# Identity first, two-transfer B loads, last values in three pieces, unequal output halves: four small changes to a decode-attention kernel that is bound by its DMA stream

## The chip, the cores and the metric

The kernel runs on one core of one Trainium2 chip. The metric is the device time of one execution in microseconds (us); the profile's span, from the first instruction to the last, is about 1.8 us shorter. The time before was 440.04 us, median of 3 runs (439.99 to 440.07).

## The reference, cut to what matters

Two attention layers decode one token each for a batch of 4, with 32 query heads, 8 key/value heads and head size 128. Layer A attends to all 8192 cached positions, layer B to the last 2048. The results stand side by side in the output.

```python
# A: whole cache; B: the same with k_cache[:, :, Sk-W:], v_cache[:, :, Sk-W:], W = 2048
q = (x @ wq).reshape(B, Sq, Hq, Dh)...           # B=4, Sq=1, D=512, Hq=32, Dh=128
scores = einsum("bhqd,bhkd->bhqk", q, k) * Dh**-0.5
o = einsum("bhqk,bhkd->bhqd", softmax(scores), v)
return o.reshape(B, Sq, Hq*Dh) @ wo
```

Nearly all bytes are the two caches, read once: 184.6 MB from HBM in all.

## The kernel before

The work is cut into 20 units, each with 4 MiB of keys and 4 MiB of values: first 4 of layer B (one per batch entry, all 8 heads), then 16 of layer A (one batch entry and two heads). K and V have two slots each. All large loads are issued by SyncE (SP) in one order: query weights of B and A, K(0), then K(u), V(u-1) in turn, at the end the last values and the last output weights (Wl). The cuts are marked by "...".

```python
# GpSimd's fills, in program order
op("pool", pool_mask0, inc=("mk0",)); op("pool", pool_mask1, inc=("mka",))
def pool_setup0(pool):
    ...memset onesf, onesb, RQ, OT_sb, oacc, PT, Wo_sb...
op("pool", pool_setup0, waits=[("mk0",), ("mka",)], inc=("pset",))
def pool_setup1(pool): ...affine_select ident, identf...
op("pool", pool_setup1, waits=[("pset",)], inc=("setup",))
...
# loads of a B unit: four transfers of 1 MiB, 128 partitions each
for q in range(NSEG):
    src = bass.AP(..., ap=[[TS * DH, 64], [SK * DH, 2], [1, TS * DH]])
    w = [("T", tjob_idx[(u - 2, 4 * q + 3)])] if u >= 2 else []      # keys
    op("sp", dma(buf[:, slot, q * TS:(q + 1) * TS, :], src), waits=w, ...)
...
# the tail: last unit's weighted values (PV) in 8 groups, each waits for its piece of V
VCH = [2, 2, 2, 1, 1]             # pieces of 1, 1, 1, 0.5, 0.5 MiB
for c in range(NC):
    if c == 4: pe_SM(L); ...seed the two output halves with oacc...
    pe_PV(L, c, bank=KTB[0], waits=[("VL", vch_of[c])])
...
H2 = D // 2                       # final projection: 8 heads x 2 halves
for hq in range(8):
    for hf in (1, 0): matmul(out=halves[hf], ..., rhs=Wl_sb[:, hq, hf*H2:(hf+1)*H2])
vector copies half 0 -> SyncE sends it; scalar copies half 1 -> ScalarE sends it
for i in range(3): sp.wait_ge(out i landed)
```

## Time and profile before

| | before |
|---|---|
| device time, median | 440.04 us |
| profile span | 438.2 us |
| read from HBM | 184.56 MB, 421 GB/s over the span |
| the big DMA queue's packets, share of 16 engines' span | 99.2% |
| TensorE busy | 83% |

From the profile page: the row of DMA busy tenths and of GB/s in 40 equal slices of the span, the packet line, and the line of the big queue.

```profile
DMA  8999999999999999999999999999999999999996
GB/s 336 432 413 422 419 419 420 421 446 406 447 431 431 416 445 431 431 431 431 431 431 431 431 431 431 431 431 431 405 456 431 431 428 431 434 431 407 449 404 256
DMA packets 13396, 184.75 MB, mean 422 GB/s; under 512 B 1428, under 2 KB 2504, under 8 KB 4552
...
q1 hardware_dynamic: 13296, 184.56, 99.2%
```

The DMA engines are full (9 tenths) in every slice but the first and last (8 and 6 tenths). From these rows I estimate that nothing that the compute engines do in between moves the end, as long as they ask for the next load in time.

Busy times by stretch (start and end in us, length, then busy us and instruction counts of PE, PEld, DVE, ACT and POOL, then granted clock, DMA share, GB/s). The first stretch holds the loads of B units, the second those of A units:

```profile
34.00:92.00 58.00, 54.97 (x1044) 51.72 (x1047) 30.59 (x56) 29.91 (x32) 2.24 (x7) 1.00 1.02 422
110.00:390.00 280.00, 241.19 (x4630) 223.97 (x4636) 143.35 (x298) 129.15 (x137) 12.83 (x47) 0.95 1.01 431
```

B's packets are 8 KB, A's are 32 KB. The start, from the timeline (start us, length us, engine, line, operation, output and inputs, count, and in brackets the idle time before and what ended it):

```profile
5.43 3.51 POOL L538 MEMSET Wo_sb<- 128x4096 bf16 x1
19.43 0.28 POOL L542 TENSOR_SCALAR_AFFINE_SELECT ident<-onesb 128x128 bf16<-128x128 bf16 x1 [10.49 <-issue]
...
20.74 3.56 PE L221 MATMUL KT<-xT,V_sb 128*128 128x4 bf16 x128 [0.37 <-ACT xT L204]
...
24.33 4.90 SPq L567 DMA_DIRECT2D V_sb<-in_B_v_cache_dram  x4
```

GpSimd fills until about 9 us, shows no instruction for 10.5 us, and then makes the identity matrix (`ident`, with which TensorE transposes). The first projections on TensorE wait for it. The first values load of B goes out at 24.33 us, behind them.

The tail, from the timeline. L324 is PV, L700 the final projection, L705 and L704 the copies of the two output halves:

```profile
422.99 3.91 PE L324 MATMUL OT<-PT,V_sb 128*128 128x64 bf16 x128 [0.64 <-DMA V_sb<-in_A_v_cache_dram]
...
428.23 1.98 PE L324 MATMUL KT<-PT,V_sb 128*128 128x64 bf16 x64 [1.33 <-issue]
...
431.55 2.10 PE L324 MATMUL KT<-PT,V_sb 128*128 128x64 bf16 x64
433.69 0.18 DVE L489 TENSOR_TENSOR OT_sb<-KT,RL 128x8 bf16<-128x8 f32 x1 [2.05 <-PE KT L324]
...
433.97 0.27 PE L700 MATMUL KT<-Wl_sb,OT_sb 128*4 128x256 bf16 x1 [0.31 <-issue]
...
435.75 0.27 PE L700 MATMUL KT<-Wl_sb,OT_sb 128*4 128x256 bf16 x1
...
436.05 0.37 ACT L705 ACTIVATE osb<-KT 4x256 bf16<-4x256 f32 x1 [9.71 <-PE KT L700]
436.16 0.41 DVE L704 CAST osb<-SA 4x256 bf16<-4x256 f32 x1 [2.30 <-PE SA L700]
436.46 0.27 ACTq L567 DMA_DIRECT2D out_dram<-osb  x1
436.60 0.28 SPq L567 DMA_DIRECT2D out_dram<-osb  x1
```

PV of the last unit but one starts when its values have landed (422.94 us in the trace's semaphore records). PV of the last unit runs in two stretches of four groups without a visible wait. Then come 16 projection matmuls, two copies, two output transfers. The projection waits a little for its weights, from the waits list (engine, line, releaser, total us, times, longest):

```profile
PEld KT L700 <- DMA Wl_sb<-in_A_wo_dram: 0.6, 3, 0.2
```

### The profile page before, as it was taken

What the parts mean: (1) busy time and instruction counts of PE and PEld (TensorE: products, weight loads), DVE (VectorE), ACT (ScalarE), POOL (GpSimd) and SP (SyncE); (2) the same over time, 40 slices, a digit from 0 to 9 for tenths busy, and PEclk for the clock granted to TensorE, in tenths of its full rate; (3) what the DMA queues carried; (4) which work ended last, traced back from release to release, by engine and by line L of the source; (5) the groups of instructions that cost most, each with busy time, mean ns of one, the idle gap of its engine ahead of it and who ended that gap; (6) DMA issues with size and microseconds to landing.
All of it is one profiled execution on the core that took longest, in us unless ns stands there. A gap on an engine that the chain in (4) does not pass through costs nothing.

```text
span 438.2 us, 15448 instructions
## 1 busy us (share of the span) xinstructions
PE 363.7 (83%) x7134; PEld 336.2 (77%) x7144; DVE 207.8 (47%) x423; ACT 193.3 (44%) x217; POOL 29.1 (7%) x96
## 2 busy tenths in 40 slices
PE   0168898998998959896989598969878895989996
PEld 0158897997997949795979588868868794979975
DVE  0003455664574634563456246625644563456651
ACT  1024473573653625371635254434635361536530
POOL 7200000000000000000000000000100000000000
PEclk9999999999999997999899699989998999799999
DMA  8999999999999999999999999999999999999996
GB/s 336 432 413 422 419 419 420 421 446 406 447 431 431 416 445 431 431 431 431 431 431 431 431 431 431 431 431 431 405 456 431 431 428 431 434 431 407 449 404 256
DMA packets 13396, 184.75 MB, mean 422 GB/s; under 512 B 1428, under 2 KB 2504, under 8 KB 4552
## 3 DMA queue, kind: packets, MB, share of 16 engines
q1 hardware_dynamic: 13296, 184.56, 99.2%
q8 instruction: 8, 0.13, 0.1%
q14 instruction: 4, 0.03, 0.0%
q0 software_dynamic: 64, 0.02, 0.0%
q10 hardware_dynamic: 24, 0.01, 0.0%
HBM read 184.56 MB, written 0.01 MB: 421 GB/s over the span
## 4 chain that ended last, share of the span: by engine, by line
PE 51%; DMA 43%; issue 2%; SPq 2%; DVE 1%; PEld 1%; PEldq 0%
DMA K_sb<-in_A_k_cache_dram 29%; PE KT L277 25%; PE OT L324 10%; DMA K_sb<-in_B_k_cache_dram 7%; DMA V_sb<-in_A_v_cache_dram 7%; PE SB L308 4%; PE SA L308 4%; PE KT L388 4%; SPq L567 1%; PE SA L336 1%; DVE oacc L396 1%; PE KT L324 1%; PEld OT L324 1%; PE KT L260 0%; DVE OS L493 0%
## 5 line engine op out<-in xcount | busy, mean ns | idle before, releaser
L277 PE MATMUL KT<-identf,K_sb 128*128 128x128 f32 x1280 | 207.2, 295 | 46.2 <-DMA K_sb<-in_A_k_cache_dram 34.2
L286 ACT ACTIVATE KT_sb<-KT 128x1024 bf16<-128x1024 bf16 x160 | 163.4, 1025 | 123.0 <-PE KT L277 123.0
L277 PEld LDWEIGHTS KT<-identf,K_sb 128*128 128x128 f32 x1280 | 146.9, 149 | 51.5 <-DMA K_sb<-in_A_k_cache_dram 35.2
L285 DVE COPY KT_sb<-KT 128x512 int32<-128x512 int32 x160 | 110.5, 691 | 154.6 <-PE KT L277 153.2
L324 PE MATMUL OT<-PT,V_sb 128*128 128x64 bf16 x2560 | 78.1, 193 | 1.9 <-issue 1.3
L324 PEld LDWEIGHTS OT<-PT,V_sb 128*128 128x128 bf16 x2560 | 75.9, 98 | 2.1 <-issue 1.4
L461 ACT ACTIVATE PT<-Dt 128x512 bf16<-128x512 f32 x40 | 24.6, 632 | 84.1 <-DVE Dt L450 84.1
L308 PEld LDWEIGHTS SA<-RQc,KT_sb 128*128 128x128 bf16 x1280 | 56.9, 98 | 2.3
L308 PEld LDWEIGHTS SB<-RQc,KT_sb 128*128 128x128 bf16 x1280 | 51.1, 97 | 7.9 <-issue 4.4
L308 PE MATMUL SA<-RQc,KT_sb 128*128 128x16 bf16 x1280 | 56.3, 170 | 0.0
L308 PE MATMUL SB<-RQc,KT_sb 128*128 128x16 bf16 x1280 | 52.8, 170 | 0.0
L412 DVE TENSOR_REDUCE M<-SB 128x8 f32<-128x512 f32 (+1 forms) x20 | 13.8, 692 | 49.9 <-PE SB L308 49.9
L433 POOL PARTITION_ALL_REDUCE MB<-M1m x20 | 7.7, 387 | 335.1 <-DVE M1m L426 335.1
L388 PE MATMUL KT<-Wo_sb,OL 128*4 128x512 bf16 x80 | 18.9, 379 | 0.0
L198 PE MATMUL KT<-ident,x_sb 4*128 4x4 bf16 x8 | 0.5, 169 | 20.1 <-POOL identf L544 20.1
L198 PEld LDWEIGHTS KT<-ident,x_sb 4*128 4x128 bf16 x8 | 0.4, 111 | 20.3 <-issue 20.3
L468 DVE TENSOR_REDUCE LB<-SA 128x8 f32<-128x512 f32 (+1 forms) x20 | 13.7, 684 | 2.8 <-PE SA L336 2.8
L450 DVE TENSOR_TENSOR Dt<-SA,MBm 128x512 f32<-128x512 f32 x20 | 13.8, 691 | 0.7
L412 DVE TENSOR_REDUCE M<-SA 128x8 f32<-128x512 f32 (+1 forms) x20 | 13.6, 681 | 0.0
L450 DVE TENSOR_TENSOR Dt<-SB,MBm 128x512 f32<-128x512 f32 x20 | 13.6, 681 | 0.0
L336 PE MATMUL SA<-PT,onesb 128*128 128x128 bf16 x168 | 12.7, 218 | 0.0
L388 PEld LDWEIGHTS KT<-Wo_sb,OL 128*4 128x4 bf16 x80 | 6.0, 84 | 8.1
(73 smaller groups left out, 122.2 us busy)
## 6 DMA issues: line engine op xcount, KB each, us to landing
K_sb<-in_A_k_cache_dram SPq DMA_DIRECT2D x15, 4096.0 KB, 22.7
V_sb<-in_A_v_cache_dram SPq DMA_DIRECT2D x15, 4096.0 KB, 30.6
K_sb<-in_B_k_cache_dram SPq DMA_DIRECT2D x16, 1024.0 KB, 22.0
V_sb<-in_B_v_cache_dram SPq DMA_DIRECT2D x16, 1024.0 KB, 18.4
V_sb<-in_B_wq_dram SPq DMA_DIRECT2D x1, 4096.0 KB, 12.4
V_sb<-in_A_wq_dram SPq DMA_DIRECT2D x1, 4096.0 KB, 21.8
Wo_sb<-in_B_wo_dram SPq DMA_DIRECT2D x4, 1024.0 KB, 12.0
K_sb<-in_A_k_cache_dram SPq DMA_DIRECT2D x2, 2048.0 KB, 17.6
```

Source lines behind the costliest of these rows:

```text
L277: ins = pe.transpose(out=bkf[:, pi * 128:(pi + 1) * 128], in_=K_sbf[:, slot, t0:t0 + 2, :].rearrange("p t d -> p (t d)"), identity=identf[ ...
L285: return e.tensor_copy(out=KT_sb.bitcast(I32)[:, tj % NKT, :], in_=bkf.bitcast(I32)[:, :])
L286: return e.activation(out=KT_sb[:, tj % NKT, :], in_=bk[:, :], func=ACTF.Copy)
L308: ins = pe.matmul(out=stb[:, t % NTH * C:(t % NTH + 2) * C], lhsT=ktv[:, pi, :, e], rhs=RQc[:, u % 2, t // TS, e, :], start=(e == 0), stop ...
L324: ins = pe.matmul(out=otb[:, s * NW:s * NW + w], lhsT=V_sb[:, slot, t, :], rhs=PT[:, slot, t * C:t * C + w], start=(j == 0), stop=(j == n ...
L336: ins = pe.matmul(out=SA[u % 2][:, s * NM:(s + 1) * NM], lhsT=onesb[:, :], rhs=PT[:, u % 2, c0:c0 + NM], start=(i == 0), stop=(i == n - 1))
L388: ins = pe.matmul(out=bk[0:Bn, 0:D], lhsT=OL[:, i // REP, i % REP, :], rhs=Wo_sb[:, i // REP, i % REP, :], start=(i == 0), stop=(i == C - 1))
L412: return dve.tensor_reduce(out=M1[:, h * n:(h + 1) * n].rearrange("p (s h) -> p s h", h=C), in_=bank[:, :].rearrange("p (s j h) -> p s h j ...
L433: return pool.partition_all_reduce(MB[:, 0:n], M1m[:, 0:n], channels=128, reduce_op=ReduceOp.max)
L450: return dve.tensor_tensor(out=Dt[:, h * NTH * C:(h + 1) * NTH * C].rearrange("p (s j h) -> p s j h", s=Sh, h=C), in0=bank[:, :].rearrange ...
L461: return act.activation(out=PT[:, u % 2, a:b], in_=Dt[:, a:b], func=ACTF.Exp, scale=scale)
L468: return dve.tensor_reduce(out=LB[:, 0:n].rearrange("p (s h) -> p s h", h=C), in_=SA[u % 2][:, 0:NSEG * NM].rearrange("p (s j h) -> p s h ...
```

## The change

The intent, as far as the diff shows it: start TensorE's first work earlier; issue fewer DMAs and so fewer semaphore writes (1,429 packets of 4 bytes in the trace before); end with fewer and larger packets; and balance the two output copies, as VectorE's took 0.41 us and started later than ScalarE's 0.37 us.

```diff
-        op("pool", pool_mask0, ...); op("pool", pool_mask1, ...)
         def pool_setup0(pool):
             pool.memset(dummy...); pool.memset(onesf...)
-            pool.memset(onesb...), RQ[0], RQ[1], OT_sb, oacc, PT, Wo_sb
-        op("pool", pool_setup0, waits=[("mk0",), ("mka",)], inc=("pset",))
+            return pool.memset(onesb[:, :], 1.0)
+        op("pool", pool_setup0, inc=("ones",))
-        op("pool", pool_setup1, waits=[("pset",)], inc=("setup",))
+        op("pool", pool_setup1, waits=[("ones",)], inc=("setup",))
         op("pool", pool_perm, ...)
+        pool_zero: RQ[0], RQ[1], OT_sb, oacc, PT, Wo_sb -> ("pset",); then pool_mask0, pool_mask1
+        (the two consumers of these fills wait for "pset")
...
-        VCH = [2, 2, 2, 1, 1]
+        VCH = [4, 2, 2]
-        H2 = D // 2
+        H2 = 3 * D // 8          # half 0: 192 columns, half 1: 320
...
-                for q in range(NSEG):
-                    src ... ap=[[TS * DH, 64], [SK * DH, 2], [1, TS * DH]]
-                    keys wait for T(u-2, 4q+3)
+                for hh in range(2):
+                    src ... ap=[[TS * DH, 64], [2 * SK * DH, NSEG], [1, TS * DH]]
+                    dst = partitions hh, hh+2, ..., all four segments
+                    keys wait for T(u-2, 15)
...
-            for i in range(3):
+            for i in (1, 2, 0):
                 sp.wait_ge(out i landed)
```

(cut to its core)

More of the change, by code (lines that the diff above doesn't have):

```diff
@@ L125, in bass_concat_heads__gqa_block_cached__sliding_block_cached__decode_kernel @@
                  "out0", "out1", "out2", "Tq", "Td", "Ta", "S", "PV", "Ed", "Ea", "Eq", "vs", "sub", "exp", "otr", "otp",
-                 "ocp", "Ef", "fin0", "fin1", "ar1", "SM", "pset", "setup", "pm0", "pm1", "oc", "ocB", "mk0", "mk", "mka", "perm", "rq"]
+                 "ocp", "Ef", "fin0", "fin1", "ar1", "SM", "ones", "pset", "setup", "pm0", "pm1", "oc", "ocB", "mk0", "mk", "mka", "perm", "rq"]
         sems = {n: sm("s_" + n) for n in names}
@@ L250, in efn @@
                 return ins
-            add(dict(eng="act", fn=efn, waits=[("T", idx)], inc=("E", idx)))
+            add(dict(eng="act", fn=efn, waits=[("T", idx), ("pset",)], inc=("E", idx)))
         def pe_filler(n):
@@ L512, in pool_otp @@
             return dict(eng="pool", fn=lambda pool: pool.tensor_copy(out=OTp[:, :, :], in_=OT_sb[:, P, q, :, :]), waits=w, inc=("otp", tn))
-        def pool_mask0(pool):
-            mkv = MK[:, :].rearrange("p (g s h) -> p g s h", g=NSEG, s=2)
-            pool.memset(mkv[0:64, :, 0, :], 0.0)
-            pool.memset(mkv[0:64, :, 1, :], -BIG)
-            pool.memset(mkv[64:128, :, 0, :], -BIG)
-            return pool.memset(mkv[64:128, :, 1, :], 0.0)
-        op("pool", pool_mask0, inc=("mk0",))
-        def pool_mask1(pool):
-            pool.memset(MASK[0][0:64, 0:REP], 0.0)
-            pool.memset(MASK[0][0:64, REP:C], -BIG)
-            pool.memset(MASK[0][64:128, 0:REP], -BIG)
-            return pool.memset(MASK[0][64:128, REP:C], 0.0)
-        op("pool", pool_mask1, inc=("mka",))
         def pool_setup0(pool):
@@ L531, in pool_setup0 @@
             pool.memset(onesf[:, :], 1.0)
-            pool.memset(onesb[:, :], 1.0)
-            pool.memset(RQ[0][:, :, :, :, :], 0.0)
-            pool.memset(RQ[1][:, :, :, :, :], 0.0)
-            pool.memset(OT_sb[:, :, :, :, :], 0.0)
-            pool.memset(oacc[:, :], 0.0)
-            pool.memset(PT[:, :, :], 0.0)
-            return pool.memset(Wo_sb[:, :, :, :], 0.0)
-        op("pool", pool_setup0, waits=[("mk0",), ("mka",)], inc=("pset",))
+            return pool.memset(onesb[:, :], 1.0)
+        op("pool", pool_setup0, inc=("ones",))
         def pool_setup1(pool):
@@ L555, in bass_concat_heads__gqa_block_cached__sliding_block_cached__decode_kernel, with pool_zero, pool_mask0, pool_mask1 @@
         op("pool", pool_perm, waits=[("setup",)], inc=("perm",))
+        def pool_zero(pool):
+            pool.memset(RQ[0][:, :, :, :, :], 0.0)
+            pool.memset(RQ[1][:, :, :, :, :], 0.0)
+            pool.memset(OT_sb[:, :, :, :, :], 0.0)
+            pool.memset(oacc[:, :], 0.0)
+            pool.memset(PT[:, :, :], 0.0)
+            return pool.memset(Wo_sb[:, :, :, :], 0.0)
+        op("pool", pool_zero, inc=("pset",))
+        def pool_mask0(pool):
+            mkv = MK[:, :].rearrange("p (g s h) -> p g s h", g=NSEG, s=2)
+            pool.memset(mkv[0:64, :, 0, :], 0.0)
+            pool.memset(mkv[0:64, :, 1, :], -BIG)
+            pool.memset(mkv[64:128, :, 0, :], -BIG)
+            return pool.memset(mkv[64:128, :, 1, :], 0.0)
+        op("pool", pool_mask0, waits=[("pset",), ("perm",)], inc=("mk0",))
+        def pool_mask1(pool):
+            pool.memset(MASK[0][0:64, 0:REP], 0.0)
+            pool.memset(MASK[0][0:64, REP:C], -BIG)
+            pool.memset(MASK[0][64:128, 0:REP], -BIG)
+            return pool.memset(MASK[0][64:128, REP:C], 0.0)
+        op("pool", pool_mask1, inc=("mka",))
         for sh in range(2):
@@ L580, in bass_concat_heads__gqa_block_cached__sliding_block_cached__decode_kernel @@
             pe_job_perm(P)
-        op("pe", None, waits=[("E", perm_idx[0]), ("setup",)])
+        op("pe", None, waits=[("E", perm_idx[0]), ("pset",)])
+        op("pool", None, waits=[("mka",)])
         add(pool_rq(0))
@@ L672, in bass_concat_heads__gqa_block_cached__sliding_block_cached__decode_kernel @@
         turn[0] = None
-        H2 = D // 2
-        halves = [SA[(L + 1) % 2][0:Bn, 0:H2], KTB[2][0:Bn, 0:H2]]
+        H2 = 3 * D // 8
+        HS = [(0, H2), (H2, D)]
+        halves = [SA[(L + 1) % 2][0:Bn, 0:H2], KTB[2][0:Bn, 0:D - H2]]
         def pe_seed(pe):
@@ L678, in pe_seed @@
             for hf in range(2):
-                ins = pe.matmul(out=halves[hf], lhsT=identf[0:Bn, 0:Bn], rhs=oacc[:, hf * H2:(hf + 1) * H2], start=True, stop=False)
+                ins = pe.matmul(out=halves[hf], lhsT=identf[0:Bn, 0:Bn], rhs=oacc[:, HS[hf][0]:HS[hf][1]], start=True, stop=False)
             return ins
@@ L699, in lfn @@
                     def lfn(pe, hq=hq, hf=hf):
-                        return pe.matmul(out=halves[hf], lhsT=OT_sb[:, 0, NSEG - 1, hq, :], rhs=Wl_sb[:, hq, hf * H2:(hf + 1) * H2],
+                        return pe.matmul(out=halves[hf], lhsT=OT_sb[:, 0, NSEG - 1, hq, :], rhs=Wl_sb[:, hq, HS[hf][0]:HS[hf][1]],
                                          start=False, stop=(hq == C - 1))
@@ L715, in kv_load @@
             if un["P"] == 1:
-                for q in range(NSEG):
-                    base = cache[un["b"], 2 * q, SK - W:SK, :]
-                    src = bass.AP(tensor=base.tensor, offset=base.offset, ap=[[TS * DH, 64], [SK * DH, 2], [1, TS * DH]])
-                    if kind == "K":
-                        w = [("T", tjob_idx[(u - 2, 4 * q + 3)])] if u >= 2 else []
-                    else:
-                        w = [("otr", u - 2)] if u >= 2 else [("T", tjob_idx[(1, 1)])] if u else [("T", qp_idx[(1, NQP - 1)])]
-                    op("sp", dma(buf[:, slot, q * TS:(q + 1) * TS, :], src), waits=w, inc=(kind if q == NSEG - 1 else kind + "h", u, q))
+                if kind == "K":
+                    w = [("T", tjob_idx[(u - 2, NJ - 1)])] if u >= 2 else []
+                else:
+                    w = [("otr", u - 2)] if u >= 2 else [("T", tjob_idx[(1, 1)])] if u else [("T", qp_idx[(1, NQP - 1)])]
+                for hh in range(2):
+                    base = cache[un["b"], hh, SK - W:SK, :]
+                    src = bass.AP(tensor=base.tensor, offset=base.offset, ap=[[TS * DH, 64], [2 * SK * DH, NSEG], [1, TS * DH]])
+                    dst0 = buf[:, slot, :, :]
+                    pstr = dst0.ap[0][0]
+                    dst = bass.AP(tensor=dst0.tensor, offset=dst0.offset + hh * pstr, ap=[[2 * pstr, 64], [TS * DH, NSEG], [1, TS * DH]])
+                    op("sp", dma(dst, src), waits=w, inc=(kind, u, hh))
                 return
@@ L736, in kv_load @@
             sem = sem_of((kind, u))
-            op("sp", lambda sp: sp.sem_inc(sem, 48), waits=w, bump=(sem, 48, None))
+            op("sp", lambda sp: sp.sem_inc(sem, 16), waits=w, bump=(sem, 16, None))
             if kind == "K" and u == L:
@@ L768, in full @@
             if key[0] in ("K", "V") and len(key) == 2:
-                return (key[0], key[1], NSEG - 1 if units[key[1]]["P"] == 1 else 0)
+                return (key[0], key[1], 1 if units[key[1]]["P"] == 1 else 0)
             if key[0] == "F":
```

## The prediction

> **What bounds the kernel now.** The DMA stream. On the profile page the DMA row is at 9 tenths in every slice between the first and the last, and the one big queue's packets take 99.2% of 16 engines' span. In the trace's packet records an 8 KB packet takes 0.309 us, a 32 KB packet 1.218, a semaphore packet about 0.009, and all 16 engines run back to back from 2 to 433 us. The chain of waits names matmuls from 34 to 141 us, but the DMA rate does not dip there (about 419 GB/s, later 431), so compute only spends slack. Only DMA engine time, or the tail behind the last bytes, can move the end.
>
> **Terms of the change.**
>
> 1. *Identity first.* In the timeline its select starts at 19.43 us, after 10.5 us of idle GpSimd behind the fills; moved up it should be ready near 13 us, and the first projections end near 17 instead of 24.3 us. But the first keys land at 34.16 us, set by the 12 MiB queued, and the engines never starve meanwhile. Worth 0.
>
> 2. *B units in two transfers.* Same bytes. Packets should stay 8 KB, as source runs stay 8 KB: the Wo loads have the same form (contiguous target, cut source) and moved as 4 KB packets (the page counts 2,048 packets of 2 to 8 KB, just what those and the 512 KB value pieces need). [...] 16 transfers fewer save 16 x 0.009 = 0.15 us per engine. Keys now wait for a whole unit's transposes: K of unit 2 is issued at about 47.6 instead of from 37.9 us, but the 20 MiB ahead of it last to 52 us. Cost 0.
>
> 3. *Last values 2+1+1 MiB instead of 1+1+1+0.5+0.5.* Per engine 8 packets of 16 KB and 16 of 8 KB instead of 24 of 8 KB and 16 of 4 KB: about 0.15 us less. But the last two PV groups (0.5 us each) now both wait for the last piece, which landed at 432.97 us; I estimate a new wait of about 0.25 us, which eats most of that on PE. The final projection then stops waiting for Wl (0.6 us in the waits list) and runs at its own pace, about 0.11 us a matmul.
>
> 4. *192 and 320 columns.* Matmul columns unchanged. The DVE copy of the last half (0.41 us for 256 columns) loses about 0.07 us; ACT's gains as much but starts earlier. Worth 0 to 0.07 us.
>
> Sum: 0.2 to 0.3 us.
>
> **Predicted:** 439.75 us, 80% range 439.1 to 440.4. Faster by over 2%: 0.01. Within 2%: 0.95. Slower by over 2%: 0.04.
>
> **Right if:** about 419 GB/s in the B stage; about 290 packets of 4 bytes fewer; identity near 13 us, keys of unit 0 still landing near 34.1; last values about 0.3 us earlier; no DMA dip near 50 us; a short PE wait before the last two PV groups.
>
> **Wrong if:** [...] the B stage (80 us) could slow a lot: packets far above 0.309 us. Or packets become 32 KB, and the B stage gains up to 2 us. Or 384-byte output rows land later.

## The result, and the profile after

The changed kernel took 441.02 us (median of 6 runs, 440.74 to 441.6), the kernel before 440.06 us (6 runs, 439.99 to 440.68). The ratio is 1.0021, 95% interval 1.0008 to 1.0034: 0.2% slower, within the 2% to which the prediction had given 0.95. Ratios are the mean time of one kernel's runs over that of the other's of the same rounds, so not quite the ratio of the medians quoted. The prediction was 439.75 us with a range up to 440.4: the result lies outside, and on the other side of the time before.

The answering lines of the page:

```profile
DMA  8999999999999999999999999999999999999996
GB/s 332 426 414 422 421 417 421 422 444 407 442 436 433 411 448 430 433 427 433 430 430 430 430 433 423 433 436 433 413 441 433 430 430 430 430 433 416 440 413 224
DMA packets 12852, 184.75 MB, mean 421 GB/s; under 512 B 1144, under 2 KB 2216, under 8 KB 4008
...
q1 hardware_dynamic: 12752, 184.56, 99.0%
```

DMA is as full as before. The big queue has 544 packets fewer; packets of 4 bytes fell from 1,429 to 1,141 in the trace's packet records, so by 16 for each of the 18 transfers that the change saves (16 in the loads of B, 2 in the last values). By stretch:

```profile
34.00:92.00 58.00, 54.71 (x1052) 51.36 (x1053) 30.96 (x56) 30.07 (x32) 2.25 (x7) 1.00 1.02 422
110.00:390.00 280.00, 244.98 (x4641) 227.00 (x4639) 143.62 (x299) 128.68 (x137) 12.83 (x47) 0.93 1.01 431
```

Both rates are what they were. The start:

```profile
0.97 0.20 POOL L517 MEMSET onesb<- 128x128 bf16 x1
...
13.13 0.28 POOL L521 TENSOR_SCALAR_AFFINE_SELECT ident<-onesb 128x128 bf16<-128x128 bf16 x1 [11.95 <-issue]
...
14.44 3.55 PE L221 MATMUL KT<-xT,V_sb 128*128 128x4 bf16 x128 [0.36 <-ACT xT L204]
...
18.02 7.29 SPq L570 DMA_DIRECT2D V_sb<-in_B_v_cache_dram  x2
...
34.39 0.90 PE L277 MATMUL KT<-identf,K_sb 128*128 128x128 f32 x3 [5.75 <-DMA K_sb<-in_B_k_cache_dram]
```

The identity is ready 6.3 us earlier, the projections and the first values load follow 6.3 us earlier, and the first transposes still start at 34.39 us (34.21 before). GpSimd's pause came along and grew from 10.5 to 12 us; it now lies on the load of the first query weights from its start (issued at 0.80 us, landed at 14.11, the pause ending at 13.13). What the pause is, the trace does not show. The tail:

```profile
423.57 3.91 PE L324 MATMUL OT<-PT,V_sb 128*128 128x64 bf16 x128 [1.18 <-DMA V_sb<-in_A_v_cache_dram]
...
428.81 1.98 PE L324 MATMUL KT<-PT,V_sb 128*128 128x64 bf16 x64 [1.33 <-DMA V_sb<-in_A_v_cache_dram]
...
432.14 1.11 PE L324 MATMUL KT<-PT,V_sb 128*128 128x64 bf16 x32
...
433.53 1.11 PE L324 MATMUL KT<-PT,V_sb 128*128 128x64 bf16 x32 [0.28 <-DMA V_sb<-in_A_v_cache_dram]
434.67 0.18 DVE L489 TENSOR_TENSOR OT_sb<-KT,RL 128x8 bf16<-128x8 f32 x1 [2.45 <-PE KT L324]
...
434.95 0.30 PE L705 MATMUL KT<-Wl_sb,OT_sb 128*4 128x320 bf16 x1 [0.32 <-issue]
...
436.48 0.30 PE L705 MATMUL KT<-Wl_sb,OT_sb 128*4 128x320 bf16 x1
...
436.81 0.43 ACT L710 ACTIVATE osb<-KT 4x320 bf16<-4x320 f32 x1 [10.43 <-PE KT L705]
436.89 0.35 DVE L709 CAST osb<-SA 4x192 bf16<-4x192 f32 x1 [2.04 <-PE SA L705]
437.27 0.28 SPq L570 DMA_DIRECT2D out_dram<-osb  x1
437.27 0.27 ACTq L570 DMA_DIRECT2D out_dram<-osb  x1
```

Three differences are to be read here. PV of the last unit but one starts 0.58 us later, since its values landed later (423.53 instead of 422.94 us in the trace's semaphore records). The second stretch of the last PV is broken in two, with 0.28 us of waiting for values. And the two output transfers are now issued in the same instant, at 437.27 us.

It is useful to cut the span at the landing of the last whole values, those of the last unit but one. I call what comes before "the stream" and what comes after "the last stretch". The trace shows 16 additions to the semaphore of each large load (for the last whole values from 420.86 to 422.94 us before); I take each for one of the 16 DMA engines, and the last for the landing; "the mean engine" is the mean of the 16 times. Before: 422.94 + 15.29 us. After: 423.53 + 15.67 us. So this pair of profiles puts +0.58 us on the stream and +0.37 us on the last stretch. (Differences in this text are taken before rounding; recorded texts below can be 0.01 us off.)

### The profile page after: what moved, and what is told of

It reads as the page before. It is cut to its first block, busy times and chain, and to the rows that moved or that the text cites. A ratio compares the mean times of both kernels' runs of the same rounds, so it can differ in the third digit from the quotient of the medians.

```text
span 439.2 us, 15442 instructions
## 1 busy us (share of the span) xinstructions
PE 367.0 (84%) x7144; PEld 338.9 (77%) x7144; DVE 207.8 (47%) x423; ACT 193.2 (44%) x217; POOL 29.1 (7%) x96
## 4 chain that ended last, share of the span: by engine, by line
DMA 47%; PE 44%; PEld 4%; issue 2%; DVE 1%; SPq 1%; PEldq 0%
DMA K_sb<-in_A_k_cache_dram 34%; PE KT L277 23%; PE OT L324 9%; DMA K_sb<-in_B_k_cache_dram 7%; DMA V_sb<-in_A_v_cache_dram 5%; PE SA L308 4%; PE SB L308 4%; PE KT L388 3%; PEld KT L277 2%; SPq L570 1%; PE SA L336 1%; DVE oacc L396 1%; PEld OT L324 1%; PEld SA L308 1%; PEld SB L308 1%
## 5 line engine op out<-in xcount | busy, mean ns | idle before, releaser
L277 PE MATMUL KT<-identf,K_sb 128*128 128x128 f32 x1280 | 209.5, 298 | 45.0 <-DMA K_sb<-in_A_k_cache_dram 29.4
L277 PEld LDWEIGHTS KT<-identf,K_sb 128*128 128x128 f32 x1280 | 148.5, 150 | 50.5 <-DMA K_sb<-in_A_k_cache_dram 30.6
L221 PE MATMUL KT<-xT,V_sb 128*128 128x4 bf16 x256 | 7.1, 166 | 5.9 <-DMA V_sb<-in_A_wq_dram 5.5
```

Of the source, the lines that this page charges most:

```text
L277: ins = pe.transpose(out=bkf[:, pi * 128:(pi + 1) * 128], in_=K_sbf[:, slot, t0:t0 + 2, :].rearrange("p t d -> p (t d)"), identity=identf[ ...
```

## The experiments

Each kernel ran in 5 rounds, beside 9 runs of the kernel before on the same chip. Three theories stood at the beginning. Theory S: GpSimd's pause on top of the first query weights delays some DMA engines for good. Theory B: the two-transfer loads cost the stream something. Theory T: the cost is in the tail. The measured sums of all runs follow at the end of this section.

### 1. Each part alone

The first four kernels are the kernel before with one part of the change each, exactly the lines of the diff above.

a_ident, the identity ahead:

```diff
+ ident and identf before RQ, OT_sb, oacc, PT, Wo_sb, masks; consumers wait for "pset"
```

> Only the identity ahead of the other fills, nothing else changed. Theory S (start): the 1 us is mostly made at the start, because GpSimd's 12 us pause before the select now falls on the first query weights and delays some DMA engines, and the slowest engine carries that to the end. Then this alone is +0.4 to +0.7 us, and the query weights of B land last about 1 us later than in before (14.1 against 13.2 us). Theory B (the two-transfer loads cost it): this alone is within 0.15 us of before. Theory T (the tail costs it): the same, within 0.15.

Measured: 440.18 us against 440.01, ratio 1.0004 (0.9991 to 1.0018). The query weights of B landed last at 13.88 us, the mean engine at 13.00 instead of 12.80 us, in the direction of Theory S. But the last whole values landed at 423.01 us, against 422.94 in before. In this profile the delay of the start does not reach the end of the slowest engine. Theory S fails as the main cause.

b_two, the B units in two transfers:

```diff
-                for q in range(NSEG):  ... 1 MiB each
+                for hh in range(2):    ... 2 MiB each
```

> Only the B units in two transfers. Theory S: -0.1 to -0.2 us (fewer semaphore packets) and the last value piece lands as in before or a little earlier. Theory B: +0.4 to +0.6 us, with the landing of the last B values 0.4 to 0.5 us later (94.4 against 93.9). Theory T: within 0.15 us of before.

Measured: 440.23 us, ratio 1.0005 (0.9991 to 1.0018). No gain and no clear loss. The trace decides better than the time: from the landing of K(1) to that of V(2), five loads of 4 MiB, the mean engine took 50.21 us here and 50.20 in before. Over all 16 profiles it is 50.20 to 50.23 us with four transfers per load (mean 50.22) and 50.19 to 50.23 with two (mean 50.21). Theory B fails, and so does the saving of the prediction.

c_values, the last values in three pieces:

```diff
-        VCH = [2, 2, 2, 1, 1]
+        VCH = [4, 2, 2]
```

> Only the last values in three pieces. Theory T: +0.2 to +0.4 us, as the last two PV groups wait together for the last piece (a PE wait of about 0.3 us before them, the second half of PV ending 0.3 to 0.4 us later behind the values before). Theories S and B put nothing on it: 0 to -0.15 us from fewer packets.

Measured: 440.23 us, ratio 1.0005 (0.9991 to 1.0019). From its timeline:

```profile
431.63 1.11 PE L324 MATMUL KT<-PT,V_sb 128*128 128x64 bf16 x32
...
433.02 1.11 PE L324 MATMUL KT<-PT,V_sb 128*128 128x64 bf16 x32 [0.28 <-DMA V_sb<-in_A_v_cache_dram]
434.16 0.18 DVE L489 TENSOR_TENSOR OT_sb<-KT,RL 128x8 bf16<-128x8 f32 x1 [2.45 <-PE KT L324]
...
436.39 0.41 DVE L704 CAST osb<-SA 4x256 bf16<-4x256 f32 x1 [2.05 <-PE SA L700]
```

The wait of 0.28 us is there as predicted. From the start of the second stretch to the copy that follows it are 2.53 us here and 2.14 us before (434.16 - 431.63, 433.69 - 431.55): 0.39 us longer, not 0.28, because the two halves take 1.11 us each instead of 2.10 together, 0.12 us more. Why they do is not shown. The projection gives 0.24 us of that back by no longer waiting for Wl: counted from the landing of the last whole values, VectorE's last copy starts 13.37 us later here and 13.22 before (436.39 - 423.02, 436.16 - 422.94). Net +0.15 us, and the last stretch is 15.43 us.

d_halves, output halves of 192 and 320 columns:

```diff
-        H2 = D // 2
+        H2 = 3 * D // 8
-            for i in range(3):
+            for i in (1, 2, 0):
```

> Only the output halves of 192 and 320 columns (and the order of the three last waits). If short rows of 384 bytes take longer to land, as the changed kernel's last transfer suggests (1.43 us from issue to landing against 1.22), +0.1 to +0.2 us. If that was the two issues falling together: -0.1 to 0.05 us.

Measured: 440.73 us (440.16 to 441.23), ratio 1.0016 (1.0002 to 1.0029): the largest of the four, from the part to which I had given 0 to -0.07 us. The last stretch is 15.50 us, so 0.2 us is in the profile. By the expectation this spoke for the short rows; section 2 shows that reading to be wrong, and the size that I had given to issues falling together. In addition, three of the five executions spent 2.2 to 2.4 us outside the span, where all executions of before and of a, b and c spent 1.8 to 1.95.

### 2. Why the halves cost, and the time outside the span

e_all_but_halves, the changed kernel with this part undone:

```diff
-        H2 = 3 * D // 8
+        H2 = D // 2
-            for i in (1, 2, 0):
+            for i in range(3):
```

> The changed kernel with output halves of 256 and the old order of the last waits; the other three parts stay. If the parts add up (0.17 + 0.22 + 0.22 measured alone), +0.4 to +0.65 us against before. If the halves carry nearly all of the 1 us and the rest is chance between builds, 0 to +0.25 us. In either case the time less the profiled span stays at 1.8 to 1.9 us in every run, as in every run so far of a kernel with halves of 256.

Measured: 440.72 us against 440.33, ratio 1.0010 (0.9997 to 1.0024), with a spread from 440.02 to 441.6. The last stretch was 15.48 us, 0.19 more than before: the values' part, a little more than in c_values (15.43). But three of five executions again spent 2.2 to 2.4 us outside the span, with halves of 256. My expectation was wrong: this time does not come from the halves alone, and does not need them.

f_halves_order_kept, unequal halves, old order of waits:

```diff
-        H2 = D // 2
+        H2 = 3 * D // 8
```

> Halves of 192 and 320 with the old order of the three last waits. Theory O (the order of the waits makes the 0.45 us that some runs of the halves kernel spend outside the profiled span): all runs at 1.8 to 1.9 us outside, total +0.2 to +0.4 us. Theory G (the two output transfers are issued in the same instant and get in each other's way) and theory R (rows of 384 or 640 bytes are slow to be written): some runs again at 2.2 to 2.4 us outside, total +0.4 to +0.7 us.

Measured: 440.28 us against 440.33, ratio 1.0004 (0.9991 to 1.0018); all five runs at 1.83 to 1.88 us outside. The last stretch was 15.44 us, 0.15 more than before. Its timeline shows why:

```profile
436.09 0.43 ACT L706 ACTIVATE osb<-KT 4x320 bf16<-4x320 f32 x1 [10.29 <-PE KT L701]
436.18 0.35 DVE L705 CAST osb<-SA 4x192 bf16<-4x192 f32 x1 [2.30 <-PE SA L701]
436.55 0.27 ACTq L567 DMA_DIRECT2D out_dram<-osb  x1
436.55 0.28 SPq L567 DMA_DIRECT2D out_dram<-osb  x1
```

Both copies end together and both transfers are issued at 436.55 us. The trace's landings: ScalarE's transfer 1.25 us after its issue, SyncE's 1.43. Before, issued 0.15 us apart, they took 1.18 and 1.22. In d_halves, too, the two were issued together, and there ScalarE's took 1.41 and SyncE's 1.23. One of the two, not always the same, pays about 0.2 us. In the packet records of f ScalarE's packets lie from 437.31 to 437.48 us and SyncE's between them, from 437.35 to 437.50; in before ScalarE's lie from 437.21 to 437.31 and SyncE's after them, from 437.36 to 437.45. No run with halves of 256 has its transfers issued together, so the direct test was not made. But the seven profiles with halves of 192 and 320 (issued within 0.002 us) all show one transfer at 1.41 to 1.44 us, the 384-byte rows in four of them and the 640-byte rows in three, and the other at 1.23 to 1.26; in the eight with halves of 256 all lie at 1.17 to 1.22.

f also goes against Theories G and R as far as they were to make the time outside the span: no execution had any.

g_order_only, the order of the three last waits alone:

```diff
-            for i in range(3):
+            for i in (1, 2, 0):
```

> Only the order of the last three waits changed, halves of 256. Theory O: some runs at 2.2 to 2.4 us outside the span. Theories G and R: none, and the total within 0.15 us of before.

Measured: 440.59 us against 440.33, ratio 1.0001 (0.9987 to 1.0015); all runs at 1.79 to 1.86 us outside, so Theory O falls as well. The last stretch was 15.35 us: from the last landing to the end of the span are 0.50 us here and 0.42 before (438.81 - 438.31, 438.24 - 437.82). In all profiles it is 0.47 to 0.50 us with the new order (seven) and 0.41 to 0.42 with the old (nine), so the order itself costs about 0.07 us. This kernel showed something else. Its stream is that of before, instruction for instruction, and still its last whole values landed at 423.45 us, 0.51 us later than in before's profile. That is chance.

h_halves_swapped, 320 columns on VectorE and SyncE, 192 on ScalarE:

```diff
-        H2 = D // 2
+        H2 = 5 * D // 8
```

> Halves swapped, 320 columns on VectorE and SyncE, 192 on ScalarE; old order of waits. The two output transfers are then issued about 0.25 us apart, but rows of 640 and 384 bytes remain. Theory G: each lands about 1.2 us after its issue, all runs at 1.8 to 1.9 us outside the span, total 0 to +0.2 us (VectorE copies 64 columns more, 0.07 us). Theory R: the 384-byte transfer, now ScalarE's, takes 1.4 us and some runs are at 2.2 to 2.4 us outside.

Measured: 440.13 us against 440.33, ratio 0.9994 (0.9981 to 1.0008): nothing in the total. All runs at 1.79 to 1.88 us outside. From the timeline:

```profile
436.10 0.32 ACT L706 ACTIVATE osb<-KT 4x192 bf16<-4x192 f32 x1 [9.78 <-PE KT L701]
436.23 0.48 DVE L705 CAST osb<-SA 4x320 bf16<-4x320 f32 x1 [2.32 <-PE SA L701]
436.45 0.27 ACTq L567 DMA_DIRECT2D out_dram<-osb  x1
436.74 0.28 SPq L567 DMA_DIRECT2D out_dram<-osb  x1
```

Rows of 640 and 384 bytes are here too, but issued 0.29 us apart, and they landed 1.19 and 1.17 us after their issues, as quickly as the rows of 512 bytes did. So the size of the rows is innocent (Theory R fails). With the slow transfer of the seven profiles now of one size, now of the other, what is left is the common instant (Theory G, for the landings; not for the time outside the span). The last stretch was 15.37 us, the 0.07 us being VectorE's longer copy.

### 3. Is the late stream a cost or chance?

i_after_again, the changed kernel unaltered on another chip (no edit):

> The changed kernel unaltered, on another chip. The stretch from the landing of the last whole values (those of the last unit but one) to the end was 15.29 us in before and 15.66 in the changed kernel; that stretch comes from the last values and the output halves and should be 15.6 to 15.7 again. The stream before it: if the 0.59 us by which those values landed later is a cost of the change, they land at 423.4 to 423.6 us again and the total is +0.8 to +1.1 us. If it was chance of the execution [...], they may land anywhere from 422.9 to 423.5 and the total is +0.4 to +0.8.

Measured: 440.64 us against 440.20, ratio 1.0014 (1.0001 to 1.0028). Last stretch 15.63 us. Last whole values at 423.36 us. Between the two outcomes that I had stated: the last stretch repeats, the stream was less late.

j_before_again, the kernel before against itself (no edit):

> The kernel before, unaltered, as if it were a change: what a difference of nothing looks like. Every theory says 0; a spread of up to 0.3 us in the median or 0.5 between executions is what the other comparisons then have to be read with. The last stretch should be 15.3 us.

Measured: 439.99 us against 440.20, ratio 1.0001 (0.9987 to 1.0015), single executions from 439.95 to 440.77. Last stretch 15.30 us. A median of five can miss by 0.2 us without any cause.

k_all_but_ident, the changed kernel with the identity where it was:

```diff
+ pool_mask0, pool_mask1, pool_setup0 with all fills, then pool_setup1, as in before
```

> The changed kernel without the identity moved ahead. If the early identity costs the stream (GpSimd's pause on top of the first query weights), the values of the last unit but one land 0.3 to 0.5 us earlier than in the changed kernel, the first query weights land on average at 12.80 to 12.85 us instead of 13.00, and the total is +0.3 to +0.5 against before. If not, the total is that of the changed kernel within 0.2 us.

Measured: 440.64 us against 440.20, ratio 1.0009 (0.9996 to 1.0023). The query weights of B landed on average at 12.84 us, the last whole values at 423.07, the last stretch was 15.68 us. Two of five runs spent 2.3 to 2.4 us outside. The landing is 0.28 us earlier than i_after_again's, as the costing case said, but l_all_but_two, which has the early identity, landed as early (423.09). Against the changed kernel of the same chip (440.64) nothing is gained in the median.

l_all_but_two, the changed kernel with four transfers per B load:

```diff
-                for hh in range(2):
+                for q in range(NSEG):
```

> The changed kernel with the B units loaded in four transfers as before. If the two-transfer loads cost the stream, 0.3 to 0.5 us less than the changed kernel. If they are neutral, as eight loads of 4 MiB each showed in the landings so far (70.3 to 70.4 us for the B stage with either), the total is that of the changed kernel within 0.2 us.

Measured: 440.64 us against 440.20, ratio 1.0012 (0.9998 to 1.0026). The last whole values landed at 423.09 us, the last stretch was 15.63 us. The changed kernel's time, so the two-transfer loads are neutral once more.

m_stream_parts, identity and two-transfer loads together, tail as before:

```diff
+ the identity ahead, as in a_ident
+ two transfers per B load, as in b_two
```

> Identity ahead and B units in two transfers together, the last values and the output halves as before: the two parts that touch the DMA stream before the tail. The last stretch should be 15.3 us as in before. If the two together cost the stream, the values of the last unit but one land at 423.3 to 423.5 us and the total is +0.3 to +0.5 us. If the late stream of the changed kernel was mostly chance, they land at 422.9 to 423.2 in most executions, and the total is 0 to +0.2 us (the identity's delay of the query weights, 0.2 us in the mean engine).

Measured: 440.49 us against 440.21, ratio 1.0010 (0.9996 to 1.0024). Its profile has the last whole values at 423.06 us and a last stretch of 15.27 us. Taking 15.3 us from the spans of all five executions puts them at 423.0 to 423.6. So the two parts do not reliably make the stream late, but a small cost is not excluded.

n_after_third, the whole change once more on that chip (no edit):

> The changed kernel a third time. Last stretch 15.6 to 15.7 us. If the two stream parts cost 0.3 us or more, total +0.7 to +1.0; if they do not, +0.35 to +0.6 us, apart from executions that spend 2.2 to 2.4 us outside the span.

Measured: 440.68 us against 440.21, ratio 1.0012 (0.9999 to 1.0026), below what a cost of 0.3 us in the stream parts would have given. The last stretch was 15.70 us, with the wait of 0.28 us before the last PV groups and both output transfers issued at 437.02 us.

### The sums

| | executions | mean time, us | mean span | over 2.1 us outside the span |
|---|---|---|---|---|
| before (beside the experiments, and again) | 41 | 440.21 | 438.37 | 0 |
| changed (first comparison, again, third) | 16 | 440.90 | 438.93 | 4 |

The spans of before scatter from 438.1 to 438.9 us, those of the changed kernel from 438.6 to 439.4. Of the 0.69 us between the means, 0.56 is in the span and 0.13 outside it. Of the span, about 0.37 us is the last stretch (15.63 to 15.70 against 15.29 and 15.30 in all profiles of the two kernels); the remaining 0.2 us is the stream, an estimate from the means, about as large as the scatter of one kernel's single executions.

## Why the prediction was wrong, point by point

What bounds the kernel was read correctly. The DMA stream is full from start to end (99.2% of 16 engines' span before, 99.0% after), the B stage stayed at 422 GB/s, and the identity that came 6.3 us earlier moved nothing in the first transposes (34.21 us before, 34.39 after). What failed are the terms of the sum: steps 2 to 4 were to gain 0.2 to 0.3 us together, but step 2 gained nothing, and steps 3 and 4, with the order of the waits, made the last stretch 0.37 us longer.

**Step 1, "Worth 0".** Right about the gain. The start did have a cost that the prediction did not look for: 0.2 us of delay in the mean engine's first landing (12.80 to 13.00 us), and 12.92 to 13.01 in all seven profiles with the early identity, against 12.80 to 12.84 in the other nine. Nothing of it could be shown at the end: a_ident's landing was within 0.07 us of before's.

**Step 2, "16 transfers fewer save 16 x 0.009 = 0.15 us per engine".** Wrong: no saving shows. The packet records give each semaphore packet 0.009 us, and 288 are gone as predicted, but five B loads take 50.2 us either way, where this step would have them 0.09 us shorter. Here a record's duration was not time taken from the stream. The slow B stage feared under "Wrong if" did not come: transfers to every second partition run at the old rate (median of an 8 KB packet from 34 to 92 us 0.312 us before and after).

**Step 3, "I estimate a new wait of about 0.25 us, which eats most of that on PE".** The mechanism was right and the wait is 0.28 us. The size of the sum was wrong: the broken PV stretch costs 0.39 us (the wait, and 0.12 us more for two halves than for one stretch), the projection gives back 0.24, and the DMA saving (0.13 us in the mean engine of c_values, about 0.15 predicted) does not come on top of it, because the end hangs on the PE chain and no longer on Wl. Net +0.15 us, where the prediction's sum (0.2 to 0.3 us, less 0.15 of step 2 and up to 0.07 of step 4) left a gain of up to about 0.1.

**Step 4, "Worth 0 to 0.07 us".** This step failed in sign. The copies changed as said (VectorE 0.41 to 0.35, ScalarE 0.37 to 0.43 us), and in f SyncE's transfer is issued 0.07 us earlier after the last whole values, just the gain that was forecast. But the prediction took the two transfers' landings as fixed: it didn't count that the 0.15 us between the two issues kept them apart. Balanced, they meet, and one of them lands 0.2 us later: 15.44 us of last stretch (f) against 15.29. The order of the waits adds about 0.07 us: 15.50 (d). The prediction did warn that the 384-byte rows might land later; they did in the first profile (1.44 us), but not for their size.

**The range.** The first comparison fell on late executions: the stream was 0.58 us late in its profile, where later ones of the same kernel had 0.41 and 0.30. Even these later ones had medians (440.64 and 440.68 us) above the range. The range of 0.65 us up from the middle allowed for no such scatter between executions; I had taken the 0.08 us spread of three runs as the noise.

So: of +0.96 us in the first pair of medians, about 0.37 us is shown and repeats (values 0.14 and 0.19 in two kernels, halves 0.15, order 0.05 to 0.08). The rest is later landing in the stream and time outside the span.

**What stays open.** Which part of the stream's lateness is a cost: the mean over 16 executions leaves 0.2 us, and no part alone shows it beyond the scatter. The times of the single engines narrow it. In the changed kernel's first profile 15 of 16 engines had the last whole values by 422.91 us (422.80 before), and one came 0.61 us after them (0.14 before). The mean engine had them at 422.29 us against 422.10; over all profiles at 422.23 to 422.29 in the nine kernels with the early identity or two-transfer loads, at 422.10 to 422.28 in the seven without. So most of the 0.58 us is one engine, and g has such a straggler too (0.47 us), without any change to the stream; a cost of about 0.1 us in the mean engine is not excluded. Why one engine straggles is not shown; the packed records do not say on which engine a packet ran.

Open, too, are the 0.4 to 0.6 us outside the span. They appear in 15 of 41 executions of six kernels (the changed one, d, e, k, l, m) and in none of 30 of a, b, c, f, g, h, nor in 41 of before. They follow none of the parts: f has the halves without them, e has them without the halves. The record shows only this: all six kernels with them combine two or more of the edits (d has halves and order), the six without have one each; why is not shown. The profile does not cover that time.

No version tried beats the kernel before by more than the scatter. h_halves_swapped came out 0.06% below it, with a last stretch 0.07 us longer, so its better total is chance.

## What to carry to other kernels

In a kernel whose DMA stream is full, as this one's, check a gain counted in packet records against the landings: 288 semaphore packets fewer bought nothing measurable here, nor did an engine that started 6.3 us earlier. In a tail, a piece that lands later than the work in front of it ends can cost more than the wait (0.39 us against 0.28 here). And before balancing two paths, ask what their offset was good for: two transfers issued in the same instant cost one of them 0.2 us, more than the 0.07 us that the balance saved.
